# Residual and q, k of the first segment kept on chip, paired copies out of PSUM, and a new order of work in an attention-and-MLP kernel

## The chip, the core and the metric

The kernel runs on one core of one Trainium2 chip. The metric is the device time of one execution in microseconds; the time before is 447.72 us, the median of three runs (446.27, 447.90 and 447.72). Engines are written as in the profile: PE (TensorE), PEld (its weight loads), DVE (VectorE), ACT (ScalarE), POOL (GpSimd) and SP (SyncE, which here only issues transfers).

## The reference

One transformer block with 2,048 rows of 576 columns in bf16. The first half is a normalization, attention over 32 heads of 18 columns in four segments of 512 rows (causal within a segment) mixed with a running memory, and a projection; the second half is a normalization and an MLP of 4,608 columns. Cut to what matters:

```python
xn = layernorm(x)
q, k, v = xn @ wq, xn @ wk, xn @ wv            # 32 heads of 18, 4 segments of 512 rows
for s in range(4):
    p = softmax(q[s] @ k[s].T * 18 ** -0.5 + causal mask)
    a_mem = (phi(q[s]) @ M) / (phi(q[s]) @ z + 1e-6)   # phi(t) = t + 1 if t > 0 else exp(t)
    o[s] = g * a_mem + (1 - g) * (p @ v[s])
    M, z = M + phi(k[s]).T @ v[s], z + phi(k[s]).sum(0)
h = x + o @ wo
out = h + gelu(layernorm(h) @ w1 + b1) @ w2 + b2
```

## The kernel before

**Stages.** The rows are handled in four segments of 512, each of four tiles of 128 rows. A segment passes stage X (normalize x and transpose it to xT, in `xreg`), stage P (project to q, k and v), stage A (attention), stage M (the memory), stage B (project with wo, add x to get h, normalize h, transpose to x2T), stage C (F1: the first MLP product with its GELU into `hT`) and D (F2: the second MLP product and the addition of h and b2). The first attention, A0, has functions of its own.

**Order of the work.** The program builds a graph of some 1,770 operations with `add`. `TIMETABLE` gives each operation a place in one long order and, with its letter, the engine that does it (p, a, d, g, s for PE, ACT, DVE, POOL, SP). `schedule` walks them in that order, gives out buffers (`Buf`, `Slots`) and writes each engine's instructions in that order; each engine then works its own list strictly from the front, waiting on semaphores. Costs in `add` served the making of the timetable alone; here they set nothing but which free buffer is picked.

**PSUM.** Eight banks of 128 x 512 fp32 (`c_s`) are shared by everything: a score step takes four neighbouring banks, other work one.

**Stage X.** `layernorm` issues `bn_stats` on two halves and `bn_aggr` (L710, L711, DVE), the reciprocal root (L714, L715, POOL) and the subtraction and scaling (L724 or L726, DVE). For the first two tiles ("centred") L724 subtracts the mean alone, and the scale is applied when q, k and v leave PSUM (L628, L632). xT comes from nine transposes on PE (L738, groups TX) with copies (L630 on ACT, L634 on DVE), or, where PE is spared, by a store to DRAM (`xnd`) and transposing transfers (`flip`, L621) of 256 rows. Eight matmuls on a zeroed tile (L644) and a ninth (L648) warm PE up first.

**Stage P.** `proj9` makes one product of q, k or v for a tile with 18 matmuls of 64 rows each, in pairs (L835), into two banks of 288 columns. Each half leaves PSUM in a copy of its own (L630 on ACT or L634 on DVE) into `qk_pad` or `v_aug`; only q and k of the first two tiles are already copied whole (L628). A tile's padded q and k are stored to DRAM (`qkd`, L893), and read back by transposing transfers as `qk`; for tile 0 PE transposes them instead (L881, group TQ). For segment 0 the transposed q and k of tiles 0 and 1 lie in `qk_lo`, those of tiles 2 and 3 in `qk_hi` (a part of `w2_lo`), read back by eight transfers A0flip.

**Stage A.** Scores (L1002 in A0, L1163 later) go to four banks; ACT takes their exponential (L1005, L1167); the diagonal blocks are masked on DVE or POOL (L1015, L1018, L1176, L1178); the value products (L1034, L1189) and the memory's (L1134 in one piece or L1137 in four strips) are transposed in 32 x 32 blocks by DVE (L1048, L1143, L1197).

**Stages B to D.** `stage_B` adds x to the projection (L1241, DVE) into fp32 `h` (three buffers), normalizes it to `xn2`, repeats its first 64 columns behind the 576 (L1246, "tail"), and stores h to DRAM (`hd`). In segment 0, x2T of tiles 0 and 1 is made by PE; all others store xn2 to DRAM (`x2d`), and transposing transfers read it back, two for a whole segment (two for 256 rows in segment 0). `stage_C` reads w1 in chunks (`w1g`) for F1 (L1338 in segment 0, L1301 later); ACT and DVE evict. For D, h is loaded again as `hc`, b2 is added to it over 576 columns (L1374, fp32), F2's matmuls are at L1388, and L1400 adds hc to the product. The output leaves in transfers of a tile (144 KB), tile 15 in two halves (72 KB).

## Time and profile before

| what | before |
|---|---|
| median of three timed runs | 447.72 us |
| profiled execution: span from first to last instruction | 444.7 us |
| instructions in the span | 12,623 |
| moved by the DMA queues | 76.7 MB |
| first matmul after the span's start | 1.78 us |

Of the profiled execution the page gives the span; what lies around it is seen from the timed runs, whose median is 3.0 us longer. A group of instructions is read as: line, engine, operation, output and inputs by name, shape, count, then busy us, mean ns of one, and the idle time of the engine just before them with what ended it. A wait is read as: who waited, for whom, us in total, how often, the longest. Matmuls overlap in the array, so a mean of theirs is longer than the time from one to the next.

### The profile page before, as it was taken

The page shows a single profiled execution, that of the slowest core. Times are in us where ns is not written, and L with a number is a line of the kernel's source. Part 1 is how long each engine was busy: PE and PEld are TensorE (multiplying, and loading weights), DVE is VectorE, ACT ScalarE, POOL GpSimd, SP SyncE. Part 2 cuts the span into 40 slices and gives each one's busy share as a digit, 9 for nine tenths or more (in the row PEclk, how much of TensorE's full clock was granted, in tenths as well). Part 3 has the DMA queues.
Part 4 walks back from the last instruction along what each step waited for, and adds up shares of the span by engine and source line. Part 5 has one row for each costly group of instructions (what it writes and reads, how often), then busy time and mean ns, then how long its engine had stood idle before and what let it go on. Part 6 is the DMA issues. An engine that isn't in the chain of part 4 may idle for free.

```text
span 444.7 us, 12623 instructions
## 1 busy us (share of the span) xinstructions
PE 431.7 (97%) x5355; PEld 278.3 (63%) x5355; DVE 291.2 (65%) x636; ACT 296.7 (67%) x269; POOL 179.3 (40%) x312
## 2 busy tenths in 40 slices
PE   8888999998999999999999999999999999999997
PEld 5666677765676776664445766654457775446775
DVE  5889888999899988867777987837765121010011
ACT  5999999999878798686798966752684002556000
POOL 5776756457748435734236559440011000000010
PEclk9999999999999999999999999999999999999999
DMA  6779989999999945693863355805463461550030
GB/s 208 204 250 246 271 264 279 228 228 244 236 257 348 315 152 166 175 242 69 245 190 52 107 146 161 201 2 153 131 210 111 101 171 39 169 194 1 1 107 28
DMA packets 85274, 76.73 MB, mean 173 GB/s; under 512 B 62945, under 2 KB 72545, under 8 KB 85217
## 3 DMA queue, kind: packets, MB, share of 16 engines
q1 hardware_dynamic: 85072, 75.83, 63.3%
q8 instruction: 42, 0.69, 0.7%
q10 hardware_dynamic: 144, 0.09, 0.1%
q14 instruction: 16, 0.12, 0.1%
HBM read 42.08 MB, written 18.87 MB: 137 GB/s over the span
## 4 chain that ended last, share of the span: by engine, by line
PE 75%; DVE 7%; DMA 6%; ACT 6%; POOL 2%; issue 2%; SPq 1%; POOLq 0%; DVEq 0%; ACTq 0%
PE bank L1388 27%; PE bank L1301 21%; PE bank L835 9%; PE bank L1338 6%; DMA w1g<-in_B_w_dram 4%; PE bank L1163 3%; ACT hT L1355 3%; PE bank L1189 3%; PE bank L793 2%; DMA x<-in_A_x_dram 2%; ACT pt L1167 1%; PE bank L1002 1%; PE bank L819 1%; DVE ln L710 1%; POOL pt L1178 1%
## 5 line engine op out<-in xcount | busy, mean ns | idle before, releaser
L1167 ACT ACTIVATE pt<-bank 128x2048 bf16<-128x2048 f32 x60 | 112.7, 1878 | 30.4 <-PE bank L1163 25.1
L1388 PEld LDWEIGHTS <-hT 128*128 128x128 bf16 x1152 | 110.2, 98 | 34.5 <-issue 7.0
L1301 PE MATMUL bank<-xreg,w1g 64*128 64x512 bf16 x972 | 108.0, 376 | 0.2 <-DMA w1g<-in_B_w_dram 0.2
L1301 PEld LDWEIGHTS <-w1g 64*128 64x128 bf16 x972 | 46.2, 94 | 57.1 <-issue 2.3
L1388 PE MATMUL bank<-w,hT 128*128 128x288 bf16 x576 | 78.3, 286 | 0.0
L1388 PE MATMUL bank<-w_lo,hT 128*128 128x288 bf16 x576 | 78.0, 286 | 0.0
L835 PE MATMUL bank<-hT,xreg 64*128 64x288 bf16 x864 | 58.0, 283 | 1.1 <-DVE qk_pad L634 0.6
L1306 ACT ACTIVATE hT<-bank,b_col 128x512 bf16<-128x512 f32 x36 | 22.5, 689 | 46.0 <-PE bank L1301 46.0
L1178 POOL TENSOR_SCALAR_AFFINE_SELECT pt<-pt 128x512 bf16<-128x512 bf16 x58 | 42.0, 737 | 27.1 <-ACT pt L1167 26.9
L835 PEld LDWEIGHTS <-xreg 64*128 64x128 bf16 x864 | 41.6, 94 | 14.3 <-issue 5.0
L1400 DVE TENSOR_TENSOR ot<-bank,hc 128x288 bf16<-128x288 f32 x32 | 13.8, 448 | 52.2 <-PE bank L1388 51.1
L1316 DVE TENSOR_SCALAR hT<-bank,b_col 128x512 bf16<-128x512 f32 x49 | 34.9, 742 | 18.6 <-PE bank L1301 18.5
L1374 POOL TENSOR_TENSOR hc<-hc,b_bc 128x576 f32<-128x576 f32 x9 | 11.7, 1297 | 82.0 <-DMA hc<-hd 82.0
L1005 ACT ACTIVATE pt<-bank 128x2048 bf16<-128x2048 f32 x20 | 37.6, 1880 | 2.8 <-PE bank L1002 2.1
L1338 PE MATMUL bank<-xreg,w1g 64*128 64x256 bf16 x648 | 38.3, 269 | 0.6 <-DMA w1g<-in_B_w_dram 0.6
L1338 PEld LDWEIGHTS <-w1g 64*128 64x128 bf16 x648 | 31.3, 94 | 6.4 <-issue 2.7
L1374 DVE TENSOR_TENSOR hc<-hc,b_bc 128x576 f32<-128x576 f32 x7 | 5.6, 817 | 43.8 <-DMA hc<-hd 43.8
L1321 ACT ACTIVATE hT<-hT 128x8192 bf16<-128x8192 bf16 (+2 forms) x6 | 31.8, 5321 | 1.7 <-DVE hT L1316 1.6
L1314 ACT ACTIVATE hT<-bank,b_col 128x512 bf16<-128x512 f32 x23 | 15.1, 685 | 21.9 <-PE bank L1301 21.6
L1176 DVE TENSOR_TENSOR pt<-pt,tri 128x512 bf16<-128x512 bf16 x38 | 21.5, 569 | 4.7 <-ACT pt L1167 4.7
L1163 PE MATMUL bank<-qk 32*128 32x512 bf16 (+3 forms) x384 | 23.8, 300 | 0.2
L1349 DVE TENSOR_TENSOR hT<-bank,b_col 128x512 bf16<-128x512 f32 x32 | 21.0, 681 | 3.8 <-PE bank L1338 3.4
(117 smaller groups left out, 564.1 us busy)
## 6 DMA issues: line engine op xcount, KB each, us to landing
w1g<-in_B_w_dram SPq DMA_DIRECT2D x41, 576.0 KB, 5.0
qkd<-qk_pad SPq DMA_DIRECT2D x15, 512.0 KB, 3.9
hd<-h SPq DMA_DIRECT2D x16, 288.0 KB, 3.9
hc<-hd SPq DMA_DIRECT2D x16, 288.0 KB, 3.6
w_lo<-in_B_w_dram SPq DMA_DIRECT2D x3, 864.0 KB, 7.0
w<-in_B_w_dram SPq DMA_DIRECT2D x3, 864.0 KB, 11.1
xb<-in_A_x_dram SPq DMA_DIRECT2D x16, 144.0 KB, 4.2
x2d<-xn SPq DMA_DIRECT2D x14, 160.0 KB, 2.9
```

The costliest lines, as they stand in the source:

```text
L835: nc.tensor.matmul(out=out, lhsT=xTb.t[r, k, ts], rhs=wt[r, k, :], start=(k == 0), stop=(k == ND - 1))
L1005: ex = add(ps, {"act": 1.88}, lambda e: nc.scalar.activation(out=pt.t[:], in_=st.t[:], func=ACT.Exp, scale=scale), [sc], pt, [st], table=" ...
L1163: nc.tensor.matmul(out=st.t[:, i, off:off + n_], lhsT=qk[rows, 1, kt * P:(kt + 1) * P], rhs=qk[rows, 0, kt * P:L], start=True, stop=True, ...
L1167: ex = add(ps, {"act": 1.88}, lambda e, st=st, pt=pt: nc.scalar.activation(out=pt.t[:], in_=st.t[:], func=ACT.Exp, scale=scale), [sc], pt, ...
L1176: nc.vector.tensor_tensor(out=blk, in0=blk, in1=tri[:].unsqueeze(1).to_broadcast([P, 4, P]), op=ALU.mult)
L1178: nc.gpsimd.affine_select(out=blk, in_=blk, pattern=[[0, 4], [1, P]], compare_op=ALU.is_ge, fill=0.0, base=0, channel_multiplier=-1)
L1301: nc.tensor.matmul(out=cc[w].t[:], lhsT=w1.t[rows, k, q, :], rhs=x2T[s].t[rows, k, :], start=(k == 0), stop=(k == ND - 1))
L1306: ready_f[f + w] = [add(pf - 12, {"act": 0.68}, lambda e, f=f, w=w, cc=cc: nc.scalar.activation(out=hT[:, :, f + w, :], in_=cc[w].t[:].rea ...
L1316: nc.vector.tensor_scalar(out=dst, in0=src, scalar1=b, scalar2=None, op0=ALU.add)
L1321: ge = add(2.9, {"act": 0.42 * (f1 - f0) + 0.2}, lambda e, f0=f0, f1=f1: nc.scalar.activation(out=hT[:, :, f0:f1, :], in_=hT[:, :, f0:f1, ...
L1338: nc.tensor.matmul(out=cc[w].t[:, q * 2 * P:(q + 1) * 2 * P], lhsT=w1.t[rows, k, q, :], rhs=x2T[s].t[rows, k, ts], start=(k == 0), stop=(k ...
L1388: nc.tensor.matmul(out=c.t[:, 0:HALF], lhsT=hT[:, tl // 2, f, (tl % 2) * P:(tl % 2 + 1) * P], rhs=w2_c[ch][:, f - ch * WCH, hf * HALF:(hf ...
```

## The change

1. **h in SBUF.** `h` is bf16, with six buffers; it is neither stored nor loaded again. b2 is added by half tiles into `hc` (two buffers of 288 fp32 columns).
2. **Second norm doubled.** `xn2` has 1,152 columns: the normalized row and all of it once more (the tail copy is 576 wide for 14 tiles, 64 wide for the two that PE transposes). Each of these 14 tiles is transposed from SBUF by one transfer of nine blocks of 128 x 128.
3. **q, k of segment 0 from SBUF.** Tiles 1 to 3 go from `qk_pad` into `qk_lo` and `qk_hi` by two transposing transfers each, of eight blocks. Segments 1 to 3 go through DRAM as before. Scores wait for the tiles that they read.
4. **Paired copies.** Every product of q, k and v takes two neighbouring banks and leaves in one copy of 576 columns.
5. **Half sums.** For the two centred tiles, ACT sums the right half (with `accum_out`, its output thrown into `junk`) and DVE the left; a mean is made of both, and the subtraction no longer waits for `bn_stats`.
6. **New timetable.** [...] 

```diff
-    "warm": "p 13 18 29",
+    "warm": "p 8 726 1702",
...
-    h_s = slots(3, [P, D], "h", F32)
-    hc_s = slots(2, [P, D], "hc", F32)
+    h_s = slots(6, [P, D], "h")
+    hc_s = slots(2, [P, HALF], "hc", F32)
...
-    xn2_s = slots(2, [P, XW], "xn2_")
+    xn2_s = slots(2, [P, 2 * D], "xn2_")
...
+                s1 = add(prio, {"act": 0.6}, lambda e: nc.scalar.activation(out=junk[:], in_=src()[:, HALF:D], func=ACT.Copy, accum_out=sm.t[:, 17:18]),
+                         after, sm, [xsrc], name="sum")
+                s0 = add(prio, {"dve": 0.42}, lambda e: nc.vector.reduce_sum(out=sm.t[:, 16:17], in_=src()[:, 0:HALF], axis=mybir.AxisListType.X),
+                         list(after) + [s1.after], None, [sm, xsrc], name="sum")
...
-                    cc = [Buf(c_s), Buf(c_s)]
-                    a = proj9(PE_P[s] + 0.001 * tl if s > 1 else p0, xT, tl, nm, xn_ok[s, tl], None, cc, ((0, ND),))
-                    for hf, c in enumerate(cc):
-                        first = nm == "k" and hf == 0
-                        evs[nm, hf] = copy(p0 - 0.5, 0.41, 0.46, lambda hf=hf, n=n, pad=pad: pad.t[:, hf * 4:(hf + 1) * 4, n, :, 0:Dh],
...
+                    c = Buf(c_s, width=2)
+                    a = proj9(p0, xT, tl, nm, xn_ok[s, tl], c, ((0, KT), (KT, ND)) if nm == "k" and s == tl == 0 else ((0, ND),))
+                    evs[nm] = copy(p0 - 0.5, 0.66, 0.76, lambda n=n, pad=pad: pad.t[:, :, n, :, 0:Dh].rearrange("p (h g) i d -> p h g i d", h=2),
...
+                elif tl:
+                    to, r = qk_lo if tl < 2 else qk_hi, slice((tl % 2) * P, (tl % 2 + 1) * P)
+                    for Q in range(2):
...
+                        tile_ok[Q, tl] = flip(p0 - 0.6, lambda Q=Q, to=to, r=r: to[:, 4 * Q:4 * Q + 4, :, r].rearrange("p g n t -> p (g n) t"),
+                                              lambda Q=Q, pad=pad: pad.t[:, 4 * Q:4 * Q + 4].rearrange("p g n i d -> p (g n i d)"), 8,
...
-                h_ok[t] = load(p0 + 0.5, lambda t=t: hd[t * P:(t + 1) * P, :], lambda h=h: h.t[:], 295e3, [prev], use=[h])
...
+                         lambda e, xn2=xn2, w=w: VEC[e].tensor_copy(out=xn2.t[:, D:D + w], in_=xn2.t[:, 0:w]), [ap], None, [xn2], name="tail")
+                h_ok[t] = h, prev
+                if by_dma:
+                    x2_ok[s].append(flip(p0, lambda tl=tl: x2T[s].t[:, :, tl * P:(tl + 1) * P], lambda xn2=xn2: xn2.t[:], ND,
...
-                    l1 = load(p2 - 10, lambda hc=hc: hc.t[:], lambda t=t: hd[t * P:(t + 1) * P, :], 295e3, [h_ok[t]], acq=hc)
...
+                hc.op = add(p2, {"dve": 0.42, "pool": 0.72}, lambda e, hc=hc, h=h, cs=cs: VEC[e].tensor_tensor(
+                    out=hc.t[:], in0=h.t[:, cs], in1=b2_bc[:, cs], op=ALU.add), [h_in, b2_ok], hc, [h], name="hc")
```

The order on ACT, from the second exponential of A0 on. Before (L1005 is an exponential, L630 a copy of half a product, L900 the exponential of k for the memory):

```order
L1005 ACTIVATE pt_72<-bank 128x2048
L900 ACTIVATE ek_87<-qk_pad_130 128x576
L630 CAST qk_pad_130<-bank 128x4x4x18
L630 CAST qk_pad_131<-bank 128x4x4x18
L630 CAST v_aug_109<-bank 128x16x18
L630 CAST qk_pad_131<-bank 128x4x4x18
L630 CAST v_aug_109<-bank 128x16x18
L630 CAST qk_pad_130<-bank 128x4x4x18
L630 CAST v_aug_109<-bank 128x16x18
L900 ACTIVATE ek_87<-qk_pad_131 128x576
L630 CAST qk_pad_131<-bank 128x4x4x18
L1005 ACTIVATE pt_73<-bank 128x2048
```

After, from the first exponential on (L641 is a whole copy with the scale, L909 the exponential of k, L619 a clearing of a buffer):

```order
L1005 ACTIVATE pt_71<-bank 128x2048
L641 ACTIVATE v_aug_112<-bank,ln_103 128x32x18
L1005 ACTIVATE pt_72<-bank 128x2048
L1005 ACTIVATE pt_73<-bank 128x2048
L909 ACTIVATE ek_90<-qk_pad_134 128x576
L619 ACTIVATE fk_pad_137<-fk_pad_137 128x32x7
L1005 ACTIVATE pt_74<-bank 128x2048
L909 ACTIVATE ek_90<-qk_pad_134 128x576
L1005 ACTIVATE pt_75<-bank 128x2048
```

The eight copies between the second and the third exponential are gone from this place; most of these products are now copied whole on DVE.

The transfers that SP issues in the first microseconds, from x tile 3 on. Before (`hT` stands for weights of q, k, v that lie there; `qkd` is DRAM):

```order
L614 DMA x_65<-in_A_x_dram 128x640
L614 DMA hT<-in_A_w_dram 128x2592
L614 DMA x_65<-in_A_x_dram 128x640
L614 DMA x_64<-in_A_x_dram 128x2x640
L893 DMA qkd_143<-qk_pad_131 128x2048
L614 DMA beta_bc<-in_A_beta_dram 128x32
L614 DMA x_65<-in_A_x_dram 128x2x640
L614 DMA hT<-in_A_w_dram 128x2592
L621 DMA_TRANSPOSE qk<-qkd_143 128x4x128 x2
L614 DMA x_64<-in_A_x_dram 128x2x640
L621 DMA_TRANSPOSE qk<-qkd_143 128x4x128 x2
```

After:

```order
L625 DMA x_65<-in_A_x_dram 128x640 x2
L625 DMA hT<-in_A_w_dram 128x2592
L625 DMA beta_bc<-in_A_beta_dram 128x32
L625 DMA hT<-in_A_w_dram 128x2592
L625 DMA x_64<-in_A_x_dram 128x2x640
L625 DMA x_65<-in_A_x_dram 128x2x640
L632 DMA_TRANSPOSE qk<-qk_pad_134 128x8x128 x2
L625 DMA w1g_98<-in_B_w_dram 128x2304
L625 DMA xnd_146<-xn_141 128x640
L625 DMA w1g_99<-in_B_w_dram 128x2304
L632 DMA_TRANSPOSE w_lo<-qk_pad_133 128x8x128
```

The store of tile 1's q and k and four transposes from it have become two transposes whose source is SBUF; both x tiles stand ahead of q's weights, and v's weights and two chunks of w1 come earlier.

The last transfers that SP issues. Before:

```order
L614 DMA hc_79<-hd 128x576
L614 DMA hd<-h_78 128x576
L614 DMA hc_80<-hd 128x576
L614 DMA out_dram<-ot_81 128x576
L614 DMA out_dram<-ot_82 128x576
L614 DMA out_dram<-ot_81 128x288 x2
```

After:

```order
L625 DMA w1g_101<-in_B_w_dram 128x2304
L625 DMA out_dram<-ot_85 128x576
L625 DMA out_dram<-ot_84 128x288 x2
L625 DMA out_dram<-ot_85 128x576 x2
L625 DMA out_dram<-ot_84 128x576
```

The transfers of half a tile no longer stand last; a whole tile's does.

184 lines of the change are left out of this document (79 added, 105 removed), and 582 rows, old and new, of the table TIMETABLE.

## Prediction

> **What bounds the kernel now.** I read the page first (busy time), then the same busy times by stretches, then what TensorE waited for.
>
> ```profile
> span 444.7 us, 12623 instructions
> PE 431.7 (97%) x5355; PEld 278.3 (63%) x5355; DVE 291.2 (65%) x636; ACT 296.7 (67%) x269; POOL 179.3 (40%) x312
> ```
>
> TensorE (PE) is busy for 431.7 of 444.7 us: 13.0 us are open, and nothing that the change does on other engines can win more than these. The instructions of after show 5,346 matmuls beside 5,355, so the work itself stays. Where do the 13.0 us lie? Columns: stretch, its length, busy us of PE, PEld, DVE, ACT, POOL, clock, DMA share, GB/s.
>
> ```profile
> 0.00:40.00 40.00, 34.43 (x616) 25.04 (x617) 32.31 (x83) 32.51 (x49) 27.54 (x53) 1.00 0.80 219
> 40.00:80.00 40.00, 39.57 (x717) 29.18 (x718) 35.48 (x84) 36.76 (x35) 25.86 (x64) 1.00 1.03 273
> 80.00:120.00 40.00, 38.07 (x664) 26.44 (x660) 38.02 (x86) 37.94 (x38) 24.51 (x39) 1.00 1.03 232
> 120.00:160.00 40.00, 39.15 (x606) 27.56 (x601) 36.53 (x75) 31.51 (x27) 21.14 (x31) 1.00 0.93 275
> 400.00:445.00 45.00, 41.55 (x346) 30.68 (x342) 4.14 (x9) 7.16 (x12) 1.28 (x1) 0.99 0.12 34
> ```
>
> PE's open time is 5.6 us before 40, 0.4 to 80, 1.9 to 120, 0.9 to 160, and 3.15 behind 400 (44.7 less 41.55: the last addition and the output's transfer). What is left, 13.0 - 12.0, is about 1 us for 160 to 400. In the middle stretches VectorE (DVE) and ScalarE (ACT) are each at 95% (38.0 and 37.9 of 40) while the DMA engines are full. So the middle is held by three sides, and the second half by PE alone. What ended PE's waits:
>
> ```profile
> PE bank L644 <- DVE pt L638: 1.8, 1, 1.8
> PE bank L881 <- POOL tri L1423: 0.9, 1, 0.9
> PE bank L1002 <- DVE xreg L634: 0.9, 1, 0.9
> PE bank L1134 <- DVE t L1197: 0.8, 1, 0.8
> PE bank L1002 <- ACT pt L1005: 0.8, 2, 0.6
> PE bank L835 <- DVE qk_pad L634: 0.6, 1, 0.6
> PE bank L835 <- DVE t L1048: 0.5, 1, 0.5
> PE bank L1189 <- DVE v_aug L634: 0.5, 1, 0.5
> ```
>
> The 1.8 us are the start, and stay. The others are small waits for copies out of PSUM (xreg, qk_pad, v_aug), for transposes of attention (t) and for exponentials (pt): for DVE and ACT queues that run late, not for transfers. That is what this change works on.
>
> **The change, part by part.**
>
> *Paired copies.* A product of q, k or v leaves PSUM in one instruction instead of two halves.
>
> ```profile
> L630 ACT CAST qk_pad<-bank 128x288 bf16<-128x288 f32 x29 | 11.1, 420 | 1.0 <-PE bank L835 0.7 <-ACT e L1123 0.2
> L628 ACT ACTIVATE qk_pad<-bank,ln 128x576 bf16<-128x576 f32 x4 | 3.0, 738 | 1.0 <-PE bank L835 0.9
> L628 ACT ACTIVATE v_aug<-bank,ln 128x288 bf16<-128x288 f32 x1 | 0.5, 503 | 0.5 <-PE bank L835 0.5
> L634 DVE CAST qk_pad<-bank 128x288 bf16<-128x288 f32 x27 | 11.6, 445 | 1.6 <-PE bank L835 1.6
> L1349 DVE TENSOR_TENSOR hT<-bank,b_col 128x512 bf16<-128x512 f32 x32 | 21.0, 681 | 3.8 <-PE bank L1338 3.4
> ```
>
> On ACT the second 288 columns cost 738 - 503 = 235 ns, so a whole plain copy is estimated at 420 + 235 = 655 ns against 840 for two. On DVE, 224 more columns cost 681 - 445 = 236 ns, so 288 more cost 303 and a whole copy 750 ns against 890. By the two orders ACT had 44 plain halves (18.5 us) and now has 14 whole ones (9.2 us): 9 us less. DVE had 40 (17.8 us) and has 28 (21.0 us): 3 us more; but seven masks of segment 1 (569 ns each) move from DVE to GpSimd (POOL), which has the room (24.5 of 40 us), 4 us less. So ACT's queue becomes clearly shorter in the first 120 us, and DVE's hardly changes in sum. The reverse side: the banks of a product come free only after 655 or 750 ns, where two halves side by side took 420 and 445. That is a rival below.
>
> *q and k of segment 0, x2 and h stay in SBUF.* Median us from issue to landing:
>
> ```profile
> qkd<-qk_pad SPq DMA_DIRECT2D x15, 512.0 KB, 3.9
> hd<-h SPq DMA_DIRECT2D x16, 288.0 KB, 3.9
> hc<-hd SPq DMA_DIRECT2D x16, 288.0 KB, 3.6
> x2d<-xn SPq DMA_DIRECT2D x14, 160.0 KB, 2.9
> qk<-qkd SPq DMA_TRANSPOSE x28, 4.2
> xreg<-x2d SPq DMA_TRANSPOSE x8, 5.4
> w_lo<-qkd SPq DMA_TRANSPOSE x4, 5.9
> ```
>
> Removed are 32 transfers of 288 KB, 14 of 160 KB and 3 of 512 KB: 9.4 + 2.3 + 1.6 = 13.3 of the 76.7 MB that the DMA queues move; what the transposes read back from DRAM, they now read from SBUF. q and k of segment 0 reach attention one transfer (3.9 us) sooner, x2 2.9 us sooner. A transpose whose source is SBUF does not occur in this trace: the two rows of transposes of eight blocks from DRAM are 4.2 and 5.9 us, and I take 4.2, the row with the most of them. If it took 5.9, q and k would still come 3.9 - 1.7 = 2.2 us sooner, and x2's transposes lie under F2 of the segment before, hundreds of matmuls. On time saved directly I put nothing: PE waited for no such transfer in the rows above. What it buys is an earlier start of attention: its second and third exponential now follow each other on ACT, where eight copies stood between them.
>
> *bf16 h.* The normalization that read fp32 h took 681 ns, the one on bf16 x 597 for 640 columns, so 537 for 576: 16 times 0.14, 2.3 us less DVE. The additions of b2 become 32 halves; they lie in the second half, where DVE is idle. The doubled row makes 14 copies 576 wide instead of 64; 8 of them are POOL's. All of this is hidden under PE.
>
> ```profile
> L726 DVE TENSOR_SCALAR xn<-h,ln 128x576 bf16<-128x576 f32 x16 | 10.9, 681 | 2.5 <-POOL ln L715 1.8 <-POOL mark_pool L799 0.4
> L726 DVE TENSOR_SCALAR xn<-x,ln 128x640 bf16<-128x640 bf16 x14 | 8.3, 597 | 1.8 <-POOL ln L715 1.8
> ```
>
> *The start.* Half sums replace bn_stats and its aggregation ahead of the first subtraction.
>
> ```profile
> 1.78 3.59 PE L644 MATMUL bank<-pt 128*128 128x512 bf16 x8 [1.78 <-DVE pt L638]
> 3.29 0.82 DVE L710 BATCH_NORM_STATS2 ln<-x 128x6 f32<-128x288 bf16 x2 [1.57 <-DMA x<-in_A_x_dram]
> 4.14 0.21 DVE L711 BATCH_NORM_AGGREGATE ln<-ln 128x2 f32<-128x12 f32 x1
> 5.16 1.17 PE L738 MATMUL bank<-ident,xn 128*128 128x128 bf16 x9
> 7.64 4.58 PE L835 MATMUL bank<-hT,xreg 64*128 64x288 bf16 x72
> ```
>
> 0.82 + 0.21 become about half a sum (0.4) and a mean (0.1): the first transposes start 0.5 us sooner. But the second tile's subtraction now stands behind the whole bn_stats of the first, and the first product behind that tile's transposes, so of the 0.5 I count 0.3.
>
> *What it adds on PE's path.* Four of the eight warm-up matmuls move into the middle, where PE has no room; the order of after has 216 changes between tilings of the array where before has 210; and the last products are now of a tile whose output leaves whole.
>
> ```profile
> L1301 PE MATMUL bank<-xreg,w1g 64*128 64x512 bf16 x972 | 108.0, 376 | 0.2 <-DMA w1g<-in_B_w_dram 0.2
> 23.36 0.40 PE L1002 MATMUL bank<-qk 32*128 32x128 bf16 x16
> 23.70 2.38 PE L835 MATMUL bank<-hT,xreg 64*128 64x288 bf16 x36
> out_dram<-ot SPq DMA_DIRECT2D x3, 144.0 KB, 2.1
> out_dram<-ot SPq DMA_DIRECT2D x2, 72.0 KB, 1.6
> ```
>
> A stream of 512 columns costs 108.0 / 486 pairs = 0.22 us, so four warm-ups 0.9. The 16 score matmuls, four at a time, stream 512 columns as well, and take 0.34 to the next group: a change costs about 0.1, six of them 0.6. The output costs 2.1 - 1.6 = 0.5. Together **+2.0 us**, with nothing to hide them.
>
> **The sum.** Against the span of 444.7: +2.0 for these; -0.3 at the start; of the 4.2 us open between the start and 80 us (5.6 + 0.4 - 1.8) I take two thirds, -2.8, since they ended on copies and exponentials that now come sooner; of the 2.8 us open from 80 to 160 again somewhat over two thirds, -2.0, since ACT has 9 us less of copies by 125 us and the masks leave DVE. That is -3.1, a span of 441.6. The three runs' median, 447.72, lies 3.0 over the span, which is taken as unchanged: **444.6 us**. From none to all of the 7.0 us the sum runs from +1.7 to -5.3.
>
> **Rivals.**
>
> *All of it and more goes* (13%): with the queues short, the 7.0 us go whole and the 1 us behind 160 too: +2.0 - 0.3 - 8.0 = -6.3, 441.4 us. For it: every wait quoted is under 1 us. Against it: each has another releaser, so they don't fall together.
>
> *The waits stay* (18%). They may come from the written order and not from the load: In the first 40 us DVE gets two half sums and two means more, and five whole copies of tiles 2 and 3 where it had two halves. Then only +2.0 is left: 449.7 us, on the edge of slower.
>
> *A cold start* (7%). The first matmuls of 512 columns take 3.59 / 8 = 0.45 us, twice the later 0.22, and 18 transposes end only at 7.6. With half the warm-ups and a pause behind them, full speed may come later; 15 pairs of the first products at twice 0.127 us are +1.9, against -3.1: 446.5 us. [...]
>
> *Pairs of banks* (20%): slower. A product needs two free neighbouring banks of eight, and scores four; the banks now stay taken 0.24 us (ACT) or 0.30 us (DVE) longer. PE already waited for qk_pad and v_aug at L835 and L1189. If a third of the 48 products is waited for, 16 x 0.27 = 4.3 us come in, and half of the gain of 4.8 is lost: 2.0 - 0.3 + 4.3 - 2.4 = +3.6, 451.3 us. It decides from about 0.1 us of waiting per product (4.8 in all). Against it: the order puts scores or other products between most of them, so a bank has a microsecond to come free.
>
> *The change does not do what it says*: no transfers fewer on PE's path. This is no case of its own, since I counted nothing for them.
>
> **Chances.** The forecast has 42%, its own range 442 to 446. A measurement of this kernel can tell about 0.5%, 2.2 us. Faster by more (under 445.5): 42 + 13 = 55%. Within: the cold start and most of the waits that stay, 7 + 13 = 20%. Slower (over 450.0): the pairs and the rest of the waits that stay, 20 + 5 = 25%. The range reaches from the deep case with the spread of the runs, 440, to the pairs, 452.
>
> **What would show it.** PE's open time before 80 us from 6.0 to about 3, and from 80 to 160 from 2.8 to under 1; ACT's busy time in 80 to 120 below 37; plain copies of 576 columns at 0.65 and 0.75 us; the warm-up matmuls in the middle at 0.22 each; the last output's transfer at 2.1. Wrong would be: PE waiting at the products (L835 before) for qk_pad or v_aug many times; a wait of SyncE or PE for the new transposes; products in the first 12 us at twice 0.127 us; open time before 40 us still at 5.6.

## The result, and the profile after

| | before | after |
|---|---|---|
| median of four timed runs | 447.49 us | 449.20 us |
| profiled execution: span | 444.7 us | 446.9 us |
| moved by the DMA queues | 76.7 MB | 63.4 MB |

After stands to before as 1.0044 (95% interval 1.0028 to 1.0060): 1.7 us longer by the medians and 2.0 by the ratio, where 3.1 us shorter was forecast. It is a small slowing: it lies within the 0.5% of no change, but its interval leaves 1 out. Its place is that of the rival "the waits stay" (449.7). The profiled execution took 448.64 us, 1.7 more than its span.

The first two lines of the page of after, span and busy time:

```profile
span 446.9 us, 12491 instructions
PE 432.7 (97%) x5345; PEld 278.0 (62%) x5346; DVE 287.9 (64%) x623; ACT 298.8 (67%) x255; POOL 183.5 (41%) x320
```

PE is busy 1.0 us more than before, and its open time went from 13.0 to 14.2 us. Both together are the 2.2 us by which the span grew. By stretches (columns as before: length, then busy us of PE, PEld, DVE, ACT, POOL, clock, DMA share, GB/s):

```profile
0.00:40.00 40.00, 32.20 (x582) 21.99 (x584) 32.36 (x81) 31.50 (x38) 26.40 (x49) 1.00 0.82 197
40.00:80.00 40.00, 39.81 (x754) 29.06 (x752) 35.31 (x85) 36.49 (x36) 25.13 (x61) 1.00 0.99 235
80.00:120.00 40.00, 37.74 (x619) 26.10 (x615) 34.89 (x68) 35.49 (x28) 31.45 (x54) 1.00 0.97 212
120.00:160.00 40.00, 39.62 (x643) 27.23 (x640) 35.39 (x69) 33.73 (x27) 21.27 (x33) 1.00 0.95 265
160.00:400.00 240.00, 239.50 (x2400) 141.84 (x2398) 145.20 (x313) 153.68 (x117) 76.94 (x124) 1.00 0.44 110
400.00:447.00 47.00, 43.86 (x367) 31.80 (x363) 4.76 (x11) 7.95 (x13) 2.33 (x3) 1.00 0.05 16
```

In the first 40 us PE is open for 7.8 us instead of 5.6; that is the whole loss, and 1.9 of it lie between 20 and 40 us. From 40 to 80 it is 0.2 (0.4 before), to 120 2.3 (1.9), to 160 0.4 (0.9), to 400 0.5 (about 1). In the stretch from 80 to 120 DVE fell from 38.0 to 34.9 and ACT from 37.9 to 35.5, so there the relief on which the forecast stood did come, and PE's open time rose all the same. From 20 to 40, where most of the loss lies, only ACT was relieved, and DVE carries 1.1 us more (before first, after second):

```profile
20.00:40.00 20.00, 17.70 (x400) 13.34 (x396) 17.93 (x46) 18.64 (x30) 15.89 (x26) 1.00 0.92 231
```

```profile
20.00:40.00 20.00, 15.85 (x382) 11.52 (x380) 19.07 (x40) 16.73 (x16) 16.09 (x24) 1.00 1.01 204
```

What ended PE's waits in after:

```profile
PE bank L936 <- DVE fk_pad L913: 1.9, 1, 1.9
PE bank L657 <- DVE mhalf L621: 1.8, 1, 1.8
PE bank L761 <- DVE xn L747: 1.5, 2, 0.9
PE bank L1002 <- ACT pt L1005: 1.2, 3, 0.8
PE bank L936 <- DVE hT L1338: 1.0, 1, 1.0
PE bank L1034 <- DVE t L1048: 0.9, 1, 0.9
PE bank L851 <- ACT qk_pad L643: 0.7, 1, 0.7
```

The second row is the start, as before. The waits for copies (xreg, qk_pad, v_aug) fell from 2.0 to 1.0 us, but those for exponentials (pt) rose from 0.8 to 1.8, others are new, and the largest of these is 1.9 us at the first memory product (L936, segment 0), for DVE's `fk_pad` (L913, the features of k). The timeline of after shows how it comes about (start, duration, engine, line; in brackets the idle time before and what ended it):

```profile
28.44 4.25 POOL L1018 TENSOR_SCALAR_AFFINE_SELECT pt<-pt 128x1024 bf16<-128x1024 bf16 x3
28.58 1.58 DVE L1015 TENSOR_TENSOR pt<-pt,tri 128x1024 bf16<-128x1024 bf16 x1
...
30.09 1.64 DVE L913 SCALAR_TENSOR_TENSOR fk_pad<-ek,rk 128x576 bf16<-128x576 bf16 x1
...
31.79 0.62 PE L936 MATMUL bank<-v_aug,fk_pad 128*128 128x76 bf16 x13 [1.87 <-DVE fk_pad L913]
```

POOL masks three blocks of the first attention, 4.25 us without a pause. Beside them DVE's own mask takes 1.58 us and `fk_pad` 1.64; in before the same `fk_pad` took 0.74. The mask stands just ahead of `fk_pad` on DVE's list, and `fk_pad` ahead of the memory product, so PE stops.

The stretching itself is not new. In before, too, POOL makes thirteen of these masks, and a mask of DVE beside one of them takes 1.59 us:

```profile
33.50 1.12 POOL L1018 TENSOR_SCALAR_AFFINE_SELECT pt<-pt 128x1024 bf16<-128x1024 bf16 x1 [0.97 <-ACT pt L1005]
33.57 1.59 DVE L1015 TENSOR_TENSOR pt<-pt,tri 128x1024 bf16<-128x1024 bf16 x1
```

There PE waits 0.2 us in all for the masks of L1015. New is that three of POOL's masks follow each other beside instructions of DVE for which PE is about to wait.

### The profile page after: what moved, and what is told of

It is laid out like the page before. It is cut to its first block, busy times and chain, and to the rows that moved or that the text cites. A ratio compares the mean times of both kernels' runs of the same rounds, so it can differ in the third digit from the quotient of the medians.

```text
span 446.9 us, 12491 instructions
## 1 busy us (share of the span) xinstructions
PE 432.7 (97%) x5345; PEld 278.0 (62%) x5346; DVE 287.9 (64%) x623; ACT 298.8 (67%) x255; POOL 183.5 (41%) x320
## 4 chain that ended last, share of the span: by engine, by line
PE 87%; DVE 4%; DMA 4%; ACT 3%; issue 1%; SPq 0%; ACTq 0%; DVEq 0%
PE bank L1376 32%; PE bank L1290 22%; PE bank L851 11%; PE bank L1327 7%; PE bank L1159 4%; PE bank L1185 3%; PE bank L810 3%; DMA qkd<-qk_pad 2%; DMA w1g<-in_B_w_dram 1%; ACT pt L1005 1%; PE bank L836 1%; PE bank L1002 1%; ACT pt L1163 1%; PE bank L761 1%; DVE hT L1305 1%
## 5 line engine op out<-in xcount | busy, mean ns | idle before, releaser
L1376 PE MATMUL bank<-w,hT 128*128 128x288 bf16 x576 | 76.8, 286 | 0.0
L851 PE MATMUL bank<-hT,xreg 64*128 64x288 bf16 x864 | 59.6, 288 | 0.7 <-ACT qk_pad L643 0.7
L1295 ACT ACTIVATE hT<-bank,b_col 128x512 bf16<-128x512 f32 x36 | 22.5, 689 | 45.8 <-PE bank L1290 45.5
L851 PEld LDWEIGHTS <-xreg 64*128 64x128 bf16 x864 | 41.2, 95 | 15.4 <-issue 4.3
L1362 POOL TENSOR_TENSOR hc<-h,b_bc 128x288 f32<-128x288 bf16 x15 | 12.1, 808 | 87.7 <-DVE ot L1387 87.7
L1305 DVE TENSOR_SCALAR hT<-bank,b_col 128x512 bf16<-128x512 f32 x42 | 30.3, 745 | 24.4 <-PE bank L1290 23.2
L1005 ACT ACTIVATE pt<-bank 128x2048 bf16<-128x2048 f32 x20 | 37.5, 1876 | 4.5 <-PE bank L1002 3.0
L1303 ACT ACTIVATE hT<-bank,b_col 128x512 bf16<-128x512 f32 x30 | 19.4, 686 | 20.8 <-PE bank L1290 20.6
L1159 PE MATMUL bank<-qk 32*128 32x384 bf16 (+3 forms) x384 | 23.8, 300 | 0.8 <-ACT pt L1163 0.6
L1204 POOL TENSOR_TENSOR o_nat<-t,t 128x288 bf16<-128x288 f32 x17 | 14.5, 852 | 17.6 <-DVE t L1201 10.2
L1338 DVE TENSOR_TENSOR hT<-bank,b_col 128x512 bf16<-128x512 f32 x31 | 20.0, 675 | 2.6 <-PE bank L1327 2.6
L1193 DVE STREAM_TRANSPOSE t<-bank 128x512 f32<-128x512 f32 x24 | 17.0, 707 | 6.5 <-PE bank L1185 3.2
```

The source lines that it names most:

```text
L851: nc.tensor.matmul(out=c.t[:, w, 0:HALF], lhsT=xTb.t[r, k, ts], rhs=wt[r, k, :], start=(k == 0), stop=(k == ND - 1))
L1005: ex = add(ps, {"act": 1.88}, lambda e: nc.scalar.activation(out=pt.t[:], in_=st.t[:], func=ACT.Exp, scale=scale), [sc], pt, [st], table=" ...
L1159: nc.tensor.matmul(out=st.t[:, i, off:off + n_], lhsT=qk[rows, 1, kt * P:(kt + 1) * P], rhs=qk[rows, 0, kt * P:L], start=True, stop=True, ...
L1295: ready_f[f + w] = [add(pf - 12, {"act": 0.68}, lambda e, f=f, w=w, cc=cc: nc.scalar.activation(out=hT[:, :, f + w, :], in_=cc[w].t[:].rea ...
L1305: nc.vector.tensor_scalar(out=dst, in0=src, scalar1=b, scalar2=None, op0=ALU.add)
L1338: nc.vector.tensor_tensor(out=dst, in0=src, in1=b.unsqueeze(2).to_broadcast([P, 2, 2 * P]), op=ALU.add)
```

## The experiments

Each ratio is to before, measured beside it on the same chip, with its 95% interval. Medians of before beside these runs were 446.83 to 447.25 us, and 447.49 beside after, so medians of different experiments compare to about 0.7 us. Where not said otherwise, the edit is one to the timetable of after.

### Parts or order?

**e6, all parts in the old order.** The code of after, with before's written order as far as the parts allow (PE's order is that of before; h has seven buffers). Two of the lines:

```diff
-    "P00copy": "a47 a64 a71 d77 d126 a58 a73 a82",
+    "P00copy": "a43 a61 a71 d72 a135 a52 a59 d131",
...
-    "P01Pk": "p 109 92",
+    "P01Pk": "p 81 101",
```

> The same with paired copies, so that it differs from the one before by these alone (and from the first run by the place of tile 1's transposes and b2's additions on DVE). If whole copies cost by holding pairs of banks and by coming in one piece where two engines shared a product: 8 to 20 us over the run with halves, with PE waiting at products and scores in the first 160 us. If they cost nothing by themselves: the same time as the run with halves.

463.80 us, 1.0370 [1.0339, 1.0402].

**e5, the same without paired copies.** Two banks and two copies for each product of q, k and v, apart from q and k of the first two tiles, as in before.

```diff
-                    c = Buf(c_s, width=2)
+                    c = Buf(c_s, width=2) if s == 0 and tl < 2 else [Buf(c_s), Buf(c_s)]
...
-                c = Buf(c_s, width=2)
+                c = [Buf(c_s), Buf(c_s)]
```

> The written order of before with four parts of the change (h in SBUF, doubled norm, q and k of segment 0 from SBUF, half sums), and the copies in halves as before: on PE and ACT the orders are those of before but for the two sums. The two transposing transfers of tile 1 stand where its store to DRAM stood; b2's additions are halves on DVE, right behind the addition that frees their buffer; h has seven buffers, hc is bf16. If it was the paired copies that made the first run so slow: 446 to 449 us. If it was the transposes from SBUF, the doubled norm or h: 455 to 472.

455.26 us, 1.0179 [1.0148, 1.0209]. Between 40 and 80 us, e6 first and e5 second:

```profile
40.00:80.00 40.00, 33.46 (x580) 24.20 (x574) 28.19 (x69) 29.25 (x25) 19.63 (x43) 0.96 0.69 204
```

```profile
40.00:80.00 40.00, 38.63 (x722) 27.55 (x712) 35.47 (x86) 36.35 (x39) 25.17 (x58) 1.00 0.90 255
```

In an order that counted on half copies, the pairs cost 8.5 us: PE is open 6.5 of these 40 us instead of 1.4. The rival of the pairs of banks was right about that order in size and more. Whether banks held longer or whole copies on one engine, where two had shared a product, cost the time, the two runs do not tell apart.

**e9, e5 with tile 1's transposes behind v's weights** on SyncE.

```diff
-    "P00flip": "s 73 74",
+    "P00flip": "s 85 86",
```

> The written order of before with four parts of the change and copies in halves, as in the run of that kind before, but with the two transposing transfers of tile 1 behind the load of v's weights on SyncE, where before's first transposes stood. In that run they stood ahead of it, waited there for tile 1's copies, and v's weights came 3.7 us later: PE waited 2.5 us and the clock fell to half for one window. If this was the price of the parts in the old order: 448 to 450 us, and what is left over 447.2 is the parts' own price in that order. If more of the parts cost: 453 to 455.

452.70 us, 1.0121 [1.0098, 1.0145]. In e5 the transposes wait at the front of SyncE's queue for their `qk_pad`, and the weights' transfer behind them is issued at 17.45 us; here it is at 14.80, worth 2.6 us. The other parts still cost 5.9 us in the old order, and PE's open time is longer than in before in each of the five stretches to 400 us, by 0.4 to 1.5.

**e1, all parts in the old order, first form.** As e6, but with tile 1's transposes later still and the sums of h and b2 on POOL.

```diff
-    "P00flip": "s 73 74",
+    "P00flip": "s 88 108",
```

> All five parts of the change (h in SBUF, doubled norm, q and k of segment 0 from SBUF, paired copies, half sums) in the written order of before: PE's instructions stand exactly as before, and each moved operation stands where its counterpart stood; h has seven buffers, hc is bf16. Theory A (the new order costs, the parts are worth a little): none of the +2.0 us of fixed costs, and some of the waits in the first 160 us go: 445.0 to 447.0 us, under before's 447.5. Theory B (the parts themselves cost, above all banks held longer by whole copies): 448.5 to 450.5, with PE waiting at the products for qk_pad and v_aug. Theory C (the parts are worth nothing on PE's path, all of the difference is the order): 447.0 to 448.0.

472.26 us, 1.0547 [1.0524, 1.0571]. Masks on POOL are late (PE at L1185 waits 4.1 us in three waits for them). The run says less about the parts than about this placing; e6 took its place.

**e10, the new order without paired copies.** After, with two copies for each product (apart from q and k of the first two tiles, as in e5), the second right behind the first.

```diff
-    "P01copy": "d110 d121 a136 d93 d106 d99",
+    "P01copy": "d110 d110.3 d121 d121.3 a136 a136.3 d93 d93.3 d106 d106.3 d99 d99.3",
```

> The changed kernel, its order kept, but every product that before copied in halves copied in two halves again, one behind the other on the engine that copied the whole: ACT gets 14 x 0.185 = 2.6 us more to do, DVE 28 x 0.14 = 3.9. If banks held in pairs for 0.65 or 0.75 us cost PE time in the new order: no change or faster, 447.5 to 449.2. If the load on ACT and DVE decides there: slower, 450 to 453.

449.56 us, 1.0065 [1.0041, 1.0089]: over after by 0.4 us by the medians and 0.9 by the ratios, with intervals that overlap. From the rows of e10:

```profile
PE bank L945 <- DVE fk_pad L921: 1.8, 1, 1.8
...
80.00:120.00 40.00, 38.66 (x628) 27.56 (x624) 36.21 (x84) 36.32 (x33) 31.59 (x57) 1.00 0.95 207
```

DVE and ACT carry 1.3 and 0.8 us more in this stretch, and PE is open 1.3 us there, less than the 2.3 of after. The wait for `fk_pad` is the same. So in the new order the pairs, forecast as the largest relief, give little, if anything, and cost nothing that these runs can tell.

### The start

**e2, all eight warm-ups in front,** as in before; after has four there and four between the attentions of segments 1 and 2.

```diff
-    "warm": "p 8 726 1702",
+    "warm": "p 8 8.3 8.6",
```

> The changed kernel with all nine warm-up matmuls in front again, as before, instead of 4, 4 and 1. Cold start theory: the clock opens some 3.5 us sooner, the 44 products that took 3.83 us take 2.7 and the ten before them 0.6 instead of 1.3; the four in the middle give back 0.9 to 1.3; four more cold ones in front cost 1.8 less the 0.85 that PE stood idle: 449.2 - 1.8 - 1.1 + 0.9 = 447.2 us. If the clock follows nothing that the warm-ups do: the middle gives 1.1, the front takes 0.9: 449.0.

449.89 us, 1.0056 [1.0030, 1.0082]: not better than after. PE's waits in e2:

```profile
PE bank L1159 <- ACT pt L1163: 1.9, 2, 1.3
...
PE bank L851 <- DMA hT<-in_A_w_dram: 1.2, 1, 1.2
```

With all eight in front, the ten product matmuls from 7.02 us (L851) take 0.72 us to the next group; in after the ten from 7.00 take 1.31. The trace's clock records, which begin with full speed, begin at 10.99 us in after and at 7.38 in before. PE then overtakes q's weights, which after loads behind the x tiles, and waits 1.2 us for them: the first scores come at 15.03 us in e2, 15.43 in after and 14.87 in before. In the middle, PE stands 1.3 us waiting for an exponential where the four warm-ups had stood. By these rows they cost nothing there: they fill a wait.

**e4, the second tile's mean ahead of the first tile's bn_stats.**

```diff
-    "X00stats": "d 17 24",
+    "X00stats": "d 19.5 24",
```

> The changed kernel with the first tile's bn_stats moved behind the second tile's mean and subtraction on DVE. Theory of the written order: the second tile's xn comes 1.0 us sooner, PE's idle 0.69 us before its transposes goes: 448.5. If the clock decides the start (full speed only from about 11 us, whatever comes sooner): the transposes and products merely run slow sooner, 0.3 at most: 448.9 to 449.2.

448.42 us, 1.0023 [1.0009, 1.0037], 0.8 us under after. It is the only edit with the whole computation that came out lower, and its interval still overlaps that of after. DVE at the start, after first, e4 second:

```profile
4.74 0.81 DVE L733 BATCH_NORM_STATS2 ln<-x 128x6 f32<-128x288 bf16 x2
...
5.91 0.39 DVE L747 TENSOR_SCALAR xn<-x,ln 128x640 bf16<-128x640 bf16 x1
```

```profile
5.26 0.39 DVE L747 TENSOR_SCALAR xn<-x,ln 128x640 bf16<-128x640 bf16 x1
5.56 0.81 DVE L733 BATCH_NORM_STATS2 ln<-x 128x6 f32<-128x288 bf16 x2
```

The second tile's subtraction comes 0.65 us sooner; the forecast had named its place behind the bn_stats as a cost.

**e7 and e11, the start mended in three places:** e2 and e4, and q's weights ahead of x tiles 2 and 3 (e7, below) or between them (e11, with 28.5 in place of 22.5).

```diff
-    "X00dma": "s 38 29 23",
+    "X00dma": "s 22.5 29 23",
```

> The changed kernel with the start mended: nine warm-ups in front, the second tile's subtraction ahead of the first tile's bn_stats, and q's weights ahead of x tiles 2 and 3, for which PE stood waiting 0.7 to 1.2 us once the clock or the tile came sooner. If what PE wins at the start stays won: 449.2 - 0.8 - 0.4 - 0.7 = 447.3. If DVE and ACT, late as a whole, take it back in the next 100 us, as they did with the fk_pad moved: 448.5 to 449.5.

> The changed kernel with nine warm-ups in front, the second tile's subtraction first, and q's weights between the loads of x tiles 3 and 2, the place that they had before (in the run with them ahead of both, PE waited 2.4 us for the normalized tiles). If what PE wins at the start stays won: 449.2 - 0.8 - 0.4 = 448.0, or less by up to 0.7. If it is taken back later: 449 to 450.5, with a second wait for exponentials or memory products at 90 to 150 us.

e7: 451.73 us, 1.0103 [1.0069, 1.0137]. e11: 451.32 us, 1.0090 [1.0073, 1.0108]. The weights come in time, and the x tiles don't: PE waits 2.4 us (e7) and 1.8 (e11) for `xn` of L749. Each of the three looks right by itself; together they lose over 2 us.

### The wait at the first memory product

**e8, POOL's masks of the first attention cut to one column.** This leaves the causal mask of those blocks out.

```diff
-                            nc.gpsimd.affine_select(out=blk, in_=blk, pattern=[[0, 4], [0, 2], [1, P]], compare_op=ALU.is_ge, fill=0.0,
+                            nc.gpsimd.affine_select(out=blk[:, :, :, 0:1], in_=blk[:, :, :, 0:1], pattern=[[0, 4], [0, 2], [1, 1]], compare_op=ALU.is_ge, fill=0.0,
```

> The changed kernel with POOL's masks in the first attention cut to one column of each block, which leaves the causal mask of that attention out (the output is not the reference's); all instructions and waits stay. Theory of contention: DVE's mask of 1.58 us and the fk_pad of 1.64 us behind it ran beside POOL's masks and take 0.64 and 0.75 without them; PE's wait of 1.87 us at M0M goes, its open time from 20 to 40 us falls from 5.0 to about 2.5, and the time to 446.5 to 447.5. If POOL's masks don't slow DVE: both stay at 1.6, and the time at 449.

447.64 us, 1.0016 [0.9996, 1.0037], under after by 1.6 us by the medians and 1.3 by the ratios. The two intervals overlap a little. The timeline of e8:

```profile
28.23 0.68 DVE L1015 TENSOR_TENSOR pt<-pt,tri 128x1024 bf16<-128x1024 bf16 x1
...
28.84 0.75 DVE L913 SCALAR_TENSOR_TENSOR fk_pad<-ek,rk 128x576 bf16<-128x576 bf16 x1
...
29.31 0.95 PE L936 MATMUL bank<-v_aug,fk_pad 128*128 128x76 bf16 x16
```

Without the long masks both DVE instructions take less than half, and the sixteen memory products run through. So the 1.9 us are POOL's masks beside DVE, and not the number of instructions on DVE's list. The edit also relieves POOL itself (9.0 us busy from 20 to 40, 16.1 in after), and what that alone is worth no run separates.

**e3, `fk_pad` ahead of DVE's mask.**

```diff
-    "P01fk": "d 124 138",
+    "P01fk": "d 124 133.5",
-    "P01rk": "g 123 137",
+    "P01rk": "g 123 133.2",
```

> The changed kernel with two instructions of DVE swapped: the last fk_pad of segment 0 ahead of the mask of 1.58 us that stood before it. Theory of the written order: PE's wait of 1.87 us at the memory product M0M goes, and since PE bounds, the time falls by nearly all of it: 447.4 us. Theory of the load (DVE is late as a whole there, beside POOL's masks): the mask comes 0.8 us later, the values and transposes behind it too, and the wait comes back at the next place that DVE serves: 448.8 to 449.4.

449.51 us, 1.0051 [1.0034, 1.0067]: as after. `fk_pad` is stretched to 1.41 us and the mask behind it to 1.58; the wait at L936 falls from 1.9 to 0.4 us, and PE waits 1.2 us at L761 for the stream transpose behind the mask.

**e12, the memory product later,** with e4.

```diff
-    "M0M": "p 177 145",
-    "M0macc": "d 180 151",
+    "M0M": "p 177 156.3",
+    "M0macc": "d 180 156.6",
```

> The changed kernel with the second tile's subtraction first and, on PE, the first memory product of segment 0 behind the transposes of two x tiles that stood behind it: PE has 1.1 us of work to do while DVE, slowed beside POOL's masks, makes the last fk_pad. If the place in the order was the cause: the wait of 1.9 us shrinks to 0.8 or less, 447.3 to 447.8. If DVE's lateness is the bound: what PE does sooner there, it waits for at the next value products and exponentials, 448.2 to 449.

449.70 us, 1.0058 [1.0039, 1.0078]. PE now waits 2.0 us at the same place, for the bank that the stream transpose (L1048) frees; that one stands behind `fk_pad` on DVE.

**e17, POOL's fills ahead of its masks,** so that the masks begin 2.8 us later; and **e18, the same with e4.**

```diff
-    "memset": "d3 d4 g27 g1 d2 a60 a36 a111 a45 g290 g162 g197",
+    "memset": "d3 d4 g27 g1 d2 a60 a36 a111 a45 g290 g158.2 g197",
...
-    "eps": "g 163 405 240 298 301 404 207 403",
+    "eps": "g 158.4 405 240 298 301 404 207 403",
-    "gmz": "g 402 164 239 249",
+    "gmz": "g 402 158.6 239 249",
```

> The changed kernel with only POOL's order changed at one place: the fill of a memory block and its two small followers (1.7 us) ahead of the three masks of 4.25 us that ran beside DVE's mask and fk_pad. These masks' exponentials were long done, and the values that need them come 5 us later. Theory of contention: DVE's mask takes 0.64 and fk_pad 0.75 instead of 1.58 and 1.64, PE's wait of 1.9 us at the memory product falls to under 0.4, the window behind it no longer halves the clock: 447.2 to 448.0, as without POOL's masks (447.6). If the masks, now 1.7 us later, stretch DVE's next instructions instead, or the fill does: the wait comes back at the values or the transposes, 449 to 450.

> The same with the second tile's subtraction ahead of the first tile's bn_stats, which gave 0.8 us by itself. If the two add up: 446.4 to 447.2, level with before or a little faster. If the second is taken back as the others were: 448 to 449.

e17: 451.75 us, 1.0100 [1.0082, 1.0119]. e18: 451.51 us, 1.0105 [1.0085, 1.0125]. The timeline of e17:

```profile
30.33 0.67 DVE L1015 TENSOR_TENSOR pt<-pt,tri 128x1024 bf16<-128x1024 bf16 x1
...
30.92 0.86 DVE L913 SCALAR_TENSOR_TENSOR fk_pad<-ek,rk 128x576 bf16<-128x576 bf16 x1
...
31.24 3.61 POOL L1018 TENSOR_SCALAR_AFFINE_SELECT pt<-pt 128x1024 bf16<-128x1024 bf16 x3
...
32.73 1.10 DVE L1053 TENSOR_TENSOR r<-r,omg_q 128x16 f32<-128x16 f32 x1
...
33.87 1.30 DVE L1057 TENSOR_TENSOR o_nat<-t,r 128x288 bf16<-128x288 f32 x1
```

The mask and `fk_pad` are short now, and the stretch falls on what then stands beside POOL's masks: L1053 takes 1.10 us (0.17 in e8) and L1057 1.30 (0.46). PE waits 2.7 us behind them, and still 1.1 at L936. Moving the masks moved the wait and won nothing.

### Other links of that chain

**e13, one k copy from DVE to ACT; e14, a transpose on DVE behind `qk_pad`; e15, both with e4; e16, e14 and e4 with the copy, and a second one, on ACT.** Of the lines, the first pair is in e13, e15 and e16, the second in e14, e15 and e16, the third in e16.

```diff
-    "P01copy": "d110 d121 a136 d93 d106 d99",
+    "P01copy": "d110 a121 a136 d93 d106 d99",
-    "A03oT": "d 441 379 422 432 452",
+    "A03oT": "d 448.5 379 422 432 452",
-    "P00copy": "a47 a64 a71 d77 d126 a58 a73 a82",
+    "P00copy": "a47 a64 a71 d77 a126 a58 a73 a82",
```

> The changed kernel with one whole copy (q of tile 2, 0.74 us) given from DVE to ACT, ahead of the exponential of k that DVE's fk_pad needs. Between 20 and 40 us DVE is busy for 19.1 of 20 us and ACT for 16.7. Theory of DVE's load there: DVE comes 0.75 us sooner to its mask and fk_pad, the wait of 1.9 us at the memory product falls to about 1.1, and with it the idle time in the window whose follower ran at half clock: 448.0 to 448.5. If ACT's exponentials, 0.65 us later each, are as near to the path: 449 to 450.

> The changed kernel with one transpose on DVE (o of segment 0, which waits for a copy on POOL) moved behind the eviction of F1 that stood behind it at 93 us. Theory of the written order: DVE no longer stands still for POOL there, PE's wait of 1.0 us for that bank at the second memory product goes, perhaps the 0.4 behind it too: 448.0 to 448.4. If it is taken back at the next wait for exponentials: 449.2.

> The two before and the second tile's subtraction first, together. If the three waits are independent: 449.2 - 0.8 - 0.9 - 0.9 = 446.6, below before's 447.2 and so faster than both. If DVE and ACT are late as a whole: 448 to 449.5, and the open time of PE before 160 us stays near 16 us.

> The same with a second copy (v of tile 0, 0.82 us) given from DVE to ACT as well, ahead of the third exponential from there. If DVE's load between 20 and 40 us decides: another 0.7 us off the wait at the memory product, no window at half clock, 446.0. If ACT's is now the later one: PE waits for exponentials in its place, 447 to 449.

e13: 452.05 us, 1.0116 [1.0092, 1.0140]. e14: 449.33 us, 1.0045 [1.0028, 1.0062]. e15: 451.11 us, 1.0088 [1.0069, 1.0108]. e16: 449.74 us, 1.0057 [1.0039, 1.0075]. In e13 and e15 the wait for `fk_pad` is 2.5 and 2.9 us: the copy on ACT makes the exponential of k late, in e13 DVE waits 1.16 us for that, and all behind it on DVE comes later. In e14 the wait for `hT` falls from 1.0 to 0.7 us and that for `qk_pad` rises from 0.7 to 1.1. In e16 the wait for `fk_pad` is gone, and PE waits elsewhere, for exponentials:

```profile
PE bank L1002 <- ACT pt L1005: 1.6, 2, 0.8
PE bank L1034 <- ACT pt L1005: 1.5, 1, 1.5
```

No version was faster than before; the nearest with the whole computation is e4.

## Why the prediction was wrong

**The step that failed** is the one of the open time: "of the 4.2 us open between the start and 80 us (5.6 + 0.4 - 1.8) I take two thirds, -2.8, since they ended on copies and exponentials that now come sooner", and with it "from 80 to 160 again somewhat over two thirds, -2.0". Term by term, in the spans (444.7 to 446.9):

| term | forecast | measured |
|---|---|---|
| PE's busy time (forecast for warm-ups in the middle and changes of tiling) | +1.5 | +1.0 |
| last output | +0.5 | 0.0 |
| start, and open time to 80 us | -0.3 - 2.8 | +2.0 |
| open time 80 to 160 us | -2.0 | -0.1 |
| open time behind 160 us | 0 | -0.7 |
| sum | -3.1 | +2.2 |

The 3.0 us that the forecast put around the span set a median beside the span of one fast execution; in every run whose span is listed, of before and of the others, the time is 1.7 to 1.9 us over its span. This changes no term.

PE's busy time rose less than forecast, and for another reason: the nine warm-ups together fell from 3.9 to 3.2 us (one of them is missing in the trace), since the four in the middle run at a granted clock of 1.00 (1.04 us busy for the three that the trace has, 1.89 for the four at the start), while the products of q, k and v rose from 58.0 to 59.6. What the changes of tiling cost was not measured apart. The copies were priced rightly. Forecast were 655 and 750 ns; these are the rows of after on ACT and DVE (minimum, median, maximum ns):

```profile
L643 ACT CAST qk_pad<-bank x10: 623/642/671, 38.6 to 125.7; 128x576 bf16<-128x576 f32 x10
```

```profile
L647 DVE CAST qk_pad<-bank x18: 690/754/759, 19.8 to 124.8; 128x576 bf16<-128x576 f32 x18
```

The load that they took away came back in part. Plain copies on ACT fell from 16.3 to 8.4 us in the first 120 us, close to the 9 of the forecast, but ACT's busy time only from 107.2 to 103.5: the new order gave it more copies of xT (3.9 to 5.1), more evictions of F1 (0.8 to 2.5) and the half sums (1.3). From 20 to 40 us DVE had more to do than before.

Above all, what failed is the passage from "these engines have less to do" to "PE waits less". PE does not wait for an engine, but for one result, at the end of a chain through several queues that each work strictly from the front (v's weights, on SyncE, were issued at 17.45 us in e5 and at 14.80 in e9, by what stood ahead of them): product of k, copy, exponential on ACT and its partner on POOL, `fk_pad` on DVE, memory product. The load of the queues is an average over 40 us; the wait is set by what stands ahead of one instruction. e10 shows it from one side: more load on DVE and ACT, and no longer time that is clear of noise. e3, e12 and e16 show it from the other: each moves one link, and the wait comes up at the next one; in e13 it grows at its place. The forecast's sign that it would be wrong, open time before 40 us still at 5.6, was met at 7.8.

**The largest new wait** was foreseen by no rival. Beside POOL's masks two instructions of DVE take 1.58 and 1.64 us (0.68 and 0.75 in e8), at a place in the order where PE is about to wait: e8 takes the wait away and gains 1.3 to 1.6 us, most of the loss, and e17 shows that it follows POOL's masks. The forecast read POOL's room as free ("GpSimd (POOL), which has the room"), for seven masks of segment 1; the same reading is wrong here for the masks of the first attention, since there POOL's work beside DVE is paid for by DVE. What causes the stretching, no run shows; the traces show where it falls. L1015 and L913 in after (against e8) and L1053 and L1057 in e17 (1.10 and 1.30 us, 0.17 and 0.46 in e8), all with two tiles as inputs (`pt,tri`, `ek,rk`, `r,omg_q`, `t,r`), are longer by 0.8 to 0.9 us each, while the stream transpose of L1048 (0.70) and the reciprocal of L1052 (0.25) keep the time of e8 beside the same masks in e17. Two inputs are not the only case, though: the scaling L749 (`xn<-x,ln`, with two columns of `ln` beside the one tile) takes 1.36 us beside the masks in e13 and 0.49 in after.

**The start.** The half sums bring the first transposes 0.64 us sooner (4.52 us, 5.16 before). The timeline of PE in after:

```profile
1.78 1.89 PE L657 MATMUL bank<-pt 128*128 128x512 bf16 x4 [1.78 <-DVE mhalf L621]
4.52 1.14 PE L761 MATMUL bank<-ident,xn 128*128 128x128 bf16 x9 [0.85 <-DVE xn L747]
6.35 0.72 PE L761 MATMUL bank<-ident,xn 128*128 128x128 bf16 x5 [0.69 <-DVE xn L747]
7.00 1.38 PE L851 MATMUL bank<-hT,xreg 64*128 64x288 bf16 x10
8.31 0.61 PE L761 MATMUL bank<-ident,xn 128*128 128x128 bf16 x4
8.85 3.90 PE L851 MATMUL bank<-hT,xreg 64*128 64x288 bf16 x44
```

The ten matmuls from 7.00 to 8.31 us are five pairs of 0.26, twice the 0.127 that before's 36 pairs show from 7.64 us on (4.58 us, at a granted clock of 1.00), and 44 take 3.83 us to the next group where 2.8 would do at that pace: what the rival "a cold start" named. Its 15 pairs at twice the time, +1.9 us, no run shows; here it is these 27 pairs, 1.7 us over that pace. Its price was smaller than it seems, 0.4 us at the first scores by e2, because q's weights come next. So the start gained 0.6 us at the transposes, and by the first scores it stood 0.6 us behind before. The median of e4 is 0.8 lower. The idle 0.85 us ahead of the first transposes counts as open time, but is no lost work: in before, warm-ups ran there.

**The other rivals.** "All of it goes" did not occur. "Pairs of banks" was decisive in the old order (8.5 us between e5 and e6), and in the new one not measurably (e10). The rival that came out, "the waits stay", had the size right (449.7 for 449.2) and in part the reason, the written order. Its size is luck: it took the old waits to stay and fixed costs of 2.0 us to come in, while waits for copies halved, larger new waits came, and PE's busy time grew by 1.0.

**Where the gain went, then.** In before's order the parts cost 5.9 us without pairs (e9) and 17 with them (e6), of which up to 2.6 may lie in the place of tile 1's transposes (e9 against e5); the new timetable gives back 12 to 15. What is left is about the masks beside DVE (1.3 to 1.6 by e8) and, less surely, the start (0.8 by e4). The transfers that were saved, 13 MB, were forecast to buy no PE time directly, and no run tests them alone. The transposes from SBUF, for which the forecast took 4.2 us, landed after 3.4 us (x2), and 5.1 and 3.2 (q and k):

```profile
xreg<-xn SPq DMA_TRANSPOSE x14, 3.4
...
w_lo<-qk_pad SPq DMA_TRANSPOSE x4, 5.1
qk<-qk_pad SPq DMA_TRANSPOSE x2, 3.2
```

**What stays open.** Why the gain of e4 is lost in e11, e12, e15 and e18 is shown only in part: e12, e15 and e18 have a longer wait near 30 us, e11 one as long as after's (1.9), and the profiled executions of all four have a mean clock under 1 (0.996, 0.995, 0.992 and 0.995; last section); but so has that of e4 (0.996). Where the 5.9 us of e9 arise was not taken apart. Masks of the first attention split between POOL and DVE otherwise, or put on DVE alone, were not tried.

## What to carry to other kernels

A relief of an engine counts only where it shortens the chain that ends PE's wait: follow that chain across the queues, instruction by instruction, before a share of the open time is credited to it. An order written for certain durations has to be made anew when instructions change their length (here worth 12 us or more), and a single number moved in it by hand mostly moves the wait on to the next link. Room on GpSimd was not free beside VectorE here: what POOL masked was paid for by the instruction of VectorE that stood beside it, mostly one with two inputs (1.58 and 1.64 us instead of 0.68 and 0.75). That was cheap where TensorE hardly waited for that instruction, as in before (0.2 us), and dear where it did (1.9).

## What the runs showed of the hardware

**A half clock behind short waits.** Inside the kernels, four traces show stretches of 3.41 us over which the granted clock of TensorE is 0.50, each right behind one at 1.00. The first two rows are stretches of e17 that follow each other, and so do the third and fourth, of after:

```profile
33.18:36.60 3.42, 0.74 (x55) 0.56 (x45) 3.21 (x6) 2.35 (x2) 1.71 (x3) 1.00 1.01 241
36.60:40.01 3.41, 3.34 (x57) 2.21 (x44) 2.90 (x9) 1.71 (x2) 1.69 (x2) 0.50 1.12 129
```

```profile
28.06:31.47 3.41, 1.83 (x75) 1.24 (x70) 3.41 (x4) 2.86 (x4) 3.41 (x4) 1.00 1.14 260
31.47:34.88 3.41, 2.17 (x87) 1.89 (x87) 3.13 (x9) 2.09 (x3) 2.83 (x7) 1.00 1.25 193
```

In e17 PE is idle for 2.68 of 3.42 us, in one wait, and the next stretch has a clock of 0.50. In after the idle sum is 1.58, and the next has 1.00. Of the other stretches that were read, two were followed by 0.50 (e4, 28.52 to 31.93 us, idle sum 1.87; e13, 31.22 to 34.64, 1.91) and two by 1.00 (after, 31.47 to 34.88, 1.24; e17, 29.77 to 33.18, 1.11). The seventh is of e8, with 1.68 us busy and so 1.73 idle; it ends in 0.50, and no wait of PE in e8 is over 1.0 us but the 1.8 at the start:

```profile
30.33:33.74 3.41, 1.68 (x69) 1.29 (x70) 3.06 (x9) 3.41 (x3) 1.60 (x6) 1.00 1.00 144
33.74:37.16 3.42, 3.42 (x57) 2.33 (x44) 2.34 (x7) 2.10 (x3) 0.26 (x1) 0.50 1.28 208
```

In e4, e8, e13 and e17 the stretches are cut where 0.50 begins, in after in steps of 3.41 us from the start of its clock records. Cut so, the four with 1.73 us or more of idle sum were followed by half a clock, and the three with 1.58 or less were not; cut otherwise, after has one of 1.87 (29.77 to 33.18) with 1.00 behind it. Seven stretches do not show where a bound lies, or whether there is a sharp one; e8 shows that no single long wait was needed. Waits that lie together may then cost more than their sum. The runs of e8 give an estimate of the price. One stretch of 3.41 us at 0.50 takes 0.004 off the mean clock of 447 us, so a run at 0.996 is counted as one with one such stretch, and a run at 0.991 or 0.992 as one with two. Those at 0.999 or more have a mean of 447.0 us, those at 0.996 448.2, those at 0.991 and 0.992 450.0, so 1.2 and 1.8 us for each; the waits ahead of the stretch are in these differences, so the clock's own share is smaller. All runs of before beside the experiments have 0.999 or 1.0. After has 0.996 in two of its four, e12 in all six (0.995 or 0.996), which may be how mends that leave a like sum of waits near 30 us lose more than they gain; no run shows it by itself.
